# Nine plain units in place of eleven, and the extra weight jobs on a rhythm of 11 slots

## The chip, the cores and the metric

The kernel runs on one core of one Trainium2 chip. The metric is the device time of one execution in microseconds (us). Before the change three runs gave 1226.11, 1227.10 and 1228.48 us, median 1227.1 us. All times "at" something are counted from the start of the profiled span.

## The reference, cut to what matters

```python
# x: 2304 tokens x 512, the output of a chunked attention (chunks of 64, 8 heads of 64)
h = np.maximum(x @ w_in, 0.0)              # first layer: 512 x 2048
x = h * h @ w_out                          # 2048 x 512
p = domain_probs / (domain_probs.sum(-1, keepdims=True) + 1e-09)   # 2304 x 4
out = np.zeros((N, D))
for e in range(4):                         # second layer, four experts
    h = np.maximum(x @ w1[e], 0.0)         # 512 x 1024
    out += p[:, e:e + 1] * (h @ w2[e])     # 1024 x 512
```

Everything is float32. The kernel gets that from the matrix engine by splitting each operand into a high and a low part and adding three products (high by high, high by low, low by high).

## The kernel before, in words

**Two stages.** The first 488 us are the attention and the first layer (`mlp`, steps of 384 or 512 tokens, numbered by the loop variable `r`). The rest is the second layer. Its work is cut into 48 units: three groups of tokens (`sp`), and in each group 16 units `m` (four experts, four column blocks of 256). A unit has seven slots `u`. In each slot `c_unit` (L579) does six matmuls of 384 columns for the first product of the layer; I call them c0 to c6.

**Two kinds of unit.** Both compute the first product by a seven-product scheme of Strassen's kind, which needs sums of weight blocks. The second product is done in one of two ways. A plain unit (`n < PLAIN`) does it directly in the next unit's slots 0 to 5: `plain_unit` (L700), six groups of six matmuls of 512 columns; the order of the groups is t = 3, 4, 5, 0, 1, 2. Group t = 3 needs block A21 of the hidden layer, which is made last: L646 (VectorE adds), L648 (ScalarE, high part), L611 (VectorE, low part, `low`). The other units use seven products there as well: `d_unit` (L683), 63 matmuls of 256 columns.

**Where the weight sums come from.** Sums and splits of weights are made once, stored to DRAM (`kept`) and loaded again by later units. There are three makers. (1) `job` (L457) runs during the first layer, at the steps in `JOBS`: it loads a raw block, makes four sums on GpSimd (L472) and four high/low splits (L479 ScalarE, L481 VectorE or GpSimd), and stores them (L486). Its `yield` numbers are half steps to wait. (2) A plain unit makes the first weights of a plain unit to come: `w1_raw` (loads, L452), `w1_add` (sums, L506), `w1_split` (L543 ScalarE, L544 GpSimd), `w1_keep` (store, L547); its second weights need no sums: `w2_raw` (L499), `w2_split` (L555, L556). (3) `w1_extra` (L513) makes, within the plain units, the first weights of units 11 to 15. It is a small program over its own slots s: loads at s = 0 into the single buffer `rawx`, sums (L521, GpSimd) at the slots in `EXTRA_SUMS`, splits (L526 ScalarE, then L527) at the slots in `EXTRA_PARTS`, store (L530) at `EXTRA_KEEP`.

**What sets the order.** Nothing is scheduled by a tool: each engine runs its instructions in the order in which the loops emit them, and waits at each for what it needs. In a slot the order is: c_unit, c_finish, w1_split, w1_keep and w1_raw (u = 1), w2_split (u = 2, 3), w2_raw (u = 3), w1_add (u = 3 to 6), w1_extra, then plain_unit and its move L722. All transfers of this stage are issued by SyncE (SP), in one queue.

**c_finish (L624)** moves the products on. ScalarE copies b after c0 and c2 and d after c3 (L629). c4 overwrites b, so it waits for the copy after c2; c6 waits for L636, which reads b after c4. L638 and L640 finish block A11, L636 and L640 finish A22.

```python
    EXTRA_SUMS = {4: 0, 5: 1, 6: 2, 10: 3}                 # L533: slot -> which sum
    EXTRA_PARTS = {3: (1, nc.vector), 9: (2, nc.vector), 12: (0, nc.gpsimd), 13: (3, nc.vector)}
    EXTRA_KEEP = 14
                    if 0 <= 7 * n + u - 14 * i <= EXTRA_KEEP:       # L1045, i = 0 to 4
                        w1_extra(11 + i, 7 * n + u - 14 * i)
```

Of the kernel before, what the change touches and what calls it, by code (L numbers as in the profile page):

```python
# [33 lines left out]
NSUP = 3  # L34
LAG_A = 2
UOFF = [1, 3, 5, 16, 8, 17, 18, 19]
JOBS = [23, 26, 29, 32, 35, 44, 47, 50, 53, 56, 64, 67, 70, 73, 76, 79]
PLAIN = 11
SWAP = 67


# [5 lines left out]
def tile_kernel(ctx, tc, q, k, v, moe_w_in, moe_w_out, moe2_p, moe2_w1, moe2_w2, out):  # L47
    nc = tc.nc
# [317 lines left out]
    for sp in range(NSUP):  # L366
        if sp < NSUP - 1:
            r = [starts[2 * sp] + i * P for i in range(3)] + [starts[2 * sp + 1] + i * P for i in range(3)]
        else:
            r = [starts[NB - 1] + i * P for i in range(3)] + [starts[2 + i] + HALF for i in range(3)]  # L370
# [66 lines left out]
    NU = E * NP  # L437
# [16 lines left out]
                in_=moe2_w1[e, h0 * 2 * P:h1 * 2 * P, f0:f0 + P].rearrange("(k p) f -> p k f", p=P),  # L454
            )

    def job(which, n):  # L457

        e, j = divmod(n, NP)
        r = late["jb"].tile([P, 7, 2 * P], F32, tag="raw", name="jraw", bufs=2)  # L460
# [9 lines left out]
        yield 4  # L470
        for o, a, b, op in SUMS[which]:
            nc.gpsimd.tensor_tensor(out=r[:, o], in0=r[:, a], in1=r[:, b], op=op)  # L472
        yield 4
        c = NW // 4
        done = []
        for part in range(4):
# [53 lines left out]
                nc.sync.dma_start(out=kept[1, n][:, z], in_=ar[:, o:o + NW].bitcast(F32))  # L530

    rawx = {}
    EXTRA_SUMS = {4: 0, 5: 1, 6: 2, 10: 3}  # L533
    EXTRA_PARTS = {3: (1, nc.vector), 9: (2, nc.vector), 12: (0, nc.gpsimd), 13: (3, nc.vector)}
    EXTRA_KEEP = 14

    def w1_split(n, part):
        c = NW // 2
# [67 lines left out]
    def plain(n):  # L606
        return n < PLAIN

# [117 lines left out]
    def d_move(n, t, what):  # L726
# [10 lines left out]
        if what == "B":  # L737
            b = pb[n, t, 1]
            fresh = j == 0 or n == PLAIN
            if fresh and t == 2:  # L740
# [112 lines left out]
    with tc.manual_schedule():  # L853
# [57 lines left out]
        for i in range(4):  # L911
            early[SWAP + 5 + i] = [(w1_add, (0, i))]
            early[LEAD + NS - 8 + i] = [(w1_add, (1, i))]
        work = [(2, i) for i in range(NU)]
        going = []

        def advance(half):
# [12 lines left out]
        for r in range(LEAD + NS + LAG):  # L930
# [7 lines left out]
            run_all(do(r, "load"))  # L938
            advance(2 * r)
            if r in JOBS:  # L940
                going.append([2 * r, job(*work[JOBS.index(r)])])
                advance(2 * r)
            if r < NTILE + LAG_A:
                if r < NTILE:
# [50 lines left out]
        for n in range(NQ + 2):  # L995
# [5 lines left out]
            for u in range(7):  # L1001
                ds = [(d, at) for d, at in ((n - 1, u), (n - 2, u + 7)) if PLAIN <= d < NQ]
                if n < NQ:
                    if u == 0 and PLAIN <= n + 1 < NQ:
                        w1_load(n + 1)
                    c_unit(n, u)
                    if n == u == 0:
# [5 lines left out]
                        late["o"] = {}  # L1013
                    if n == PLAIN and u == 0:
                        raw_pool.close()
# [26 lines left out]
                if u >= 3 and n + 2 < PLAIN:  # L1042
                    w1_add(n + 2, u - 3)
                for i in range(5):
                    if 0 <= 7 * n + u - 14 * i <= EXTRA_KEEP:  # L1045
                        w1_extra(11 + i, 7 * n + u - 14 * i)
                if 0 < n <= PLAIN and u < 6:
                    t = (u + 3) % 6
                    plain_unit(n - 1, t)
# [38 lines left out]
```

## Time and profile before

| what | value |
|---|---|
| median of three runs | 1227.1 us (1226.11 to 1228.48) |
| profiled execution | 1226.38 us |
| its span | 1224.5 us |
| TensorE busy / VectorE / ScalarE / GpSimd | 98% / 67% / 49% / 58% |
| matmuls, weight loads | 8047 each |
| granted TensorE clock, mean | 0.993 |
| DRAM traffic | 189.30 MB read, 63.44 MB written |

The profiled execution is 0.7 us below the median and inside the spread of the three runs. The profile's page gives shares over the whole span; the timeline gives instructions in order of time, merged where one engine repeats a line; a bracket names what ended the idle time before an instruction. PEld is the weight load of TensorE, which runs beside its matmuls.

### The profile page before, as it was taken

Reading aid. Unit: us, or ns where it says so; the run is one execution under the profiler, and the core shown is the slowest. Engines: PE = TensorE matmul, PEld = TensorE weight load, DVE = VectorE, ACT = ScalarE, POOL = GpSimd, SP = SyncE. Lnnn points to the kernel's source line nnn. Section 1 sums busy time; section 2 is a strip of 40 time slices with the busy share of each in tenths; the row PEclk is TensorE's granted clock in tenths of the full one; section 3 lists DMA queues with packets and bytes.
Section 4 is the critical chain, followed back from the end, with each engine's and each line's share of the span. In section 5 each row is a group of like instructions: output and inputs, shape, how many; then the busy total and the mean of one; then the engine's idle time right before and its main releaser. Section 6 shows DMA issues by size and latency. Waiting matters only on the chain.

```text
span 1224.5 us, 21396 instructions
## 1 busy us (share of the span) xinstructions
PE 1196.7 (98%) x8047; PEld 1111.0 (91%) x8047; DVE 826.0 (67%) x1379; ACT 602.7 (49%) x1221; POOL 714.7 (58%) x686
## 2 busy tenths in 40 slices
PE   7899999999999999999999999999999999999997
PEld 5798888889888988888988999999999999999996
DVE  6975667656747466455555777676767776767676
ACT  5654555534534345644442556454445654545453
POOL 3410057726745455777881667667756766566665
PEclk8999999999999999999999999999999999999999
DMA  9855023552453644577767668666666686666652
GB/s 212 191 115 155 20 86 119 184 189 86 172 199 102 207 155 151 212 257 256 267 232 300 260 253 297 266 252 256 245 248 258 246 293 241 241 241 249 248 227 112
DMA packets 136230, 254.12 MB, mean 208 GB/s; under 512 B 64960, under 2 KB 110016, under 8 KB 129984
## 3 DMA queue, kind: packets, MB, share of 16 engines
q1 hardware_dynamic: 133504, 252.12, 59.1%
q8 instruction: 63, 1.03, 0.3%
q10 hardware_dynamic: 2624, 0.66, 0.3%
q14 instruction: 39, 0.32, 0.1%
HBM read 189.30 MB, written 63.44 MB: 206 GB/s over the span
## 4 chain that ended last, share of the span: by engine, by line
PE 89%; DVE 6%; ACT 1%; DMA 1%; issue 1%; POOL 1%; SPq 0%; DVEq 0%; ACTq 0%; POOLq 0%
PE pst L596 23%; PE psa L691 21%; PE psa L333 15%; PE pst L300 9%; PE psa L708 8%; PE psh L300 6%; PE psh L596 4%; PE pst L276 1%; PE pst L220 1%; PE pst L235 1%; DMA v<-in_v 1%; PE pst L262 1%; DVE o L791 1%; DVE uw L747 1%; DVE o L790 0%
## 5 line engine op out<-in xcount | busy, mean ns | idle before, releaser
L596 PE MATMUL pst<-ar 128*128 128x384 f32 x1728 | 345.6, 336 | 2.0 <-DVE psh L636 1.7
L596 PEld LDWEIGHTS pst<-ar 128*128 128x128 f32 x1728 | 293.7, 188 | 7.7 <-DVE psh L636 2.0
L333 PE MATMUL psa<-ar 128*128 128x512 f32 (+1 forms) x960 | 219.4, 372 | 1.2 <-ACT ar L316 0.4
L333 PEld LDWEIGHTS psa<-ar 128*128 128x128 f32 x960 | 173.5, 188 | 27.4 <-DVE ar L317 2.0
L622 POOL TENSOR_TENSOR ar<-s,ar 128x384 fp32r<-128x384 f32 x148 | 151.3, 1034 | 68.9 <-ACT ar L621 67.4
L691 PE MATMUL psa<-w2x,ar 128*128 128x256 f32 x1197 | 160.1, 278 | 2.5 <-DVE uw L745 2.3
L691 PE MATMUL psa<-ar 128*128 128x256 f32 x1134 | 158.0, 283 | 1.8 <-DVE uw L741 0.7
L691 PEld LDWEIGHTS psa<-w2x,ar 128*128 128x128 f32 x1197 | 154.8, 188 | 4.2 <-DVE uw L745 2.5
L691 PEld LDWEIGHTS psa<-ar 128*128 128x128 f32 x1134 | 151.2, 188 | 4.1 <-DVE uw L747 1.9
L145 POOL TENSOR_TENSOR raw<-raw 128x512 f32<-128x512 f32 x32 | 34.4, 1073 | 180.4 <-DVE raw L144 73.3
L759 POOL TENSOR_TENSOR o<-o,x 128x256 f32<-128x256 f32 x104 | 82.7, 795 | 80.3 <-ACT x L755 78.0
L300 PE MATMUL pst<-ar 128*128 128x512 f32 (+1 forms) x576 | 127.2, 369 | 0.0
L300 PEld LDWEIGHTS pst<-ar 128*128 128x128 f32 x576 | 105.4, 188 | 14.3
L629 ACT COPY u<-pst 128x384 f32<-128x384 f32 x144 | 69.7, 484 | 94.3 <-PE pst L596 92.2
L640 ACT ACTIVATE ar<-psh 128x384 fp32r<-128x384 f32 x96 | 47.3, 493 | 137.9 <-DVE psh L636 74.6
L621 ACT CAST ar<-s 128x384 fp32r<-128x384 f32 x148 | 75.8, 513 | 73.0 <-DVE s L617 67.9
L708 PE MATMUL psa<-ar 128*128 128x512 f32 x396 | 102.5, 394 | 0.0
L747 DVE TENSOR_TENSOR uw<-psa,uw 128x512 f32<-128x512 f32 x111 | 73.3, 687 | 34.6 <-PE psa L691 21.2
L300 PE MATMUL psh<-ar 128*128 128x512 f32 (+1 forms) x384 | 89.7, 376 | 2.2 <-DVE ar L284 2.2
L708 PEld LDWEIGHTS psa<-ar 128*128 128x128 f32 x396 | 73.2, 188 | 11.7 <-DVE ar L611 0.3
L745 DVE TENSOR_TENSOR uw<-psa,uw 128x512 f32<-128x512 f32 x81 | 56.0, 691 | 40.1 <-PE psa L691 39.8
L300 PEld LDWEIGHTS psh<-ar 128*128 128x128 f32 x384 | 69.0, 190 | 10.8 <-DVE ar L284 2.3
(136 smaller groups left out, 1936.0 us busy)
## 6 DMA issues: line engine op xcount, KB each, us to landing
ar<-w1d SPq DMA_DIRECT2D x37, 1792.0 KB, 7.3
w2x<-w2d SPq DMA_DIRECT2D x38, 896.0 KB, 7.6
ar<-w2d SPq DMA_DIRECT2D x36, 896.0 KB, 8.1
w2d<-jsplit SPq DMA_DIRECT2D x64, 448.0 KB, 3.5
w1d<-ar SPq DMA_DIRECT2D x11, 1792.0 KB, 8.7
w1d<-ar SPq DMA_DIRECT2D x10, 896.0 KB, 6.1
raw<-in_moe_w_in SPq DMA_DIRECT2D x16, 512.0 KB, 4.5
raw<-in_moe_w_out SPq DMA_DIRECT2D x16, 512.0 KB, 5.0
```

Source lines behind the costliest of these rows:

```text
L300: nc.tensor.matmul(ph[:, :T], lhsT=w[:, kk, :], rhs=x[tb][:, kk, :], start=(kk == 0 and n == 0), stop=(kk == KD - 1 and n == 2),)
L333: nc.tensor.matmul(o, lhsT=w, rhs=y, start=(f == 0 and n == 0), stop=(f == G - 1 and n == 2))
L596: nc.tensor.matmul(p, lhsT=w[:, kk, :], rhs=y[:, kk, :], start=(kk == 0 and z == 0 and u in (0, 1, 3)), stop=(kk == 1 and z == 2 and u in ...
L621: nc.scalar.copy(h, st[n, nm])
L622: nc.gpsimd.tensor_tensor(out=l, in0=st[n, nm], in1=h.bitcast(F32), op=ALU.subtract)
L629: nc.scalar.copy(s, d if at == 3 else b)
L640: nc.scalar.activation(out=g[n][i][0], in_=c, func=AF.Relu)
L691: nc.tensor.matmul(p, lhsT=w, rhs=y, start=(k in (1, 7) and z == 0), stop=(k in (3, 4) and z == 2), skip_group_check=True,)
L708: nc.tensor.matmul(p, lhsT=w[:, ts], rhs=y[:, i, :], start=(i == 0 and z == 0), stop=(i == 1 and z == 2))
L745: nc.vector.tensor_tensor(out=uw, in0=b, in1=uw, op=ALU.add)
L747: nc.vector.tensor_tensor(out=uw, in0=pb[n, t, 0], in1=uw, op=ALU.add)
L759: nc.gpsimd.tensor_tensor(out=o1[:, :2 * P], in0=o1[:, :2 * P], in1=x, op=ALU.add)
```

## The change

Units 9 and 10 become seven-product units. Their second weights were made by `job` before as well; their first weights are now made by two more jobs, so that the list of jobs grows from 16 to 18. In the last third of the first layer the jobs start every second step (64, 66, ... 78) and not every third, and wait two half steps and not four between sums and splits. The extra sums for units 11 to 15 take 11 slots each and not 14, and begin with unit 1 and not unit 0; the part that GpSimd split is now split on VectorE.

```diff
-JOBS = [23, 26, 29, 32, 35, 44, 47, 50, 53, 56, 64, 67, 70, 73, 76, 79]
-PLAIN = 11
+JOBS = [23, 26, 29, 32, 35, 44, 47, 50, 53, 56, 64, 66, 68, 70, 72, 74, 76, 78]
+PLAIN = 9
...
-    def job(which, n):
+    def job(which, n, lag):
...
-        yield 4
+        yield lag
...
-    EXTRA_SUMS = {4: 0, 5: 1, 6: 2, 10: 3}
-    EXTRA_PARTS = {3: (1, nc.vector), 9: (2, nc.vector), 12: (0, nc.gpsimd), 13: (3, nc.vector)}
-    EXTRA_KEEP = 14
+    EXTRA_SUMS = {3: 0, 4: 1, 5: 2, 6: 3}
+    EXTRA_PARTS = {3: (1, nc.vector), 7: (2, nc.vector), 8: (0, nc.vector), 9: (3, nc.vector)}
+    EXTRA_KEEP = 10
...
-        work = [(2, i) for i in range(NU)]
+        work = [(2, i) for i in range(12)] + [(1, 9), (2, 12), (2, 13), (1, 10), (2, 14), (2, 15)]
...
-                going.append([2 * r, job(*work[JOBS.index(r)])])
+                going.append([2 * r, job(*work[JOBS.index(r)], 4 if r < 64 else 2)])
...
-                    if 0 <= 7 * n + u - 14 * i <= EXTRA_KEEP:
-                        w1_extra(11 + i, 7 * n + u - 14 * i)
+                    if 0 <= 7 * n + u - 7 - 11 * i <= EXTRA_KEEP:
+                        w1_extra(11 + i, 7 * n + u - 7 - 11 * i)
```

Before, an extra job always began in slot 0 of a unit. Now the five begin in unit 1 slot 0, unit 2 slot 4, unit 4 slot 1, unit 5 slot 5 and unit 7 slot 2. I name each by the unit that it serves (the job for 11, for 12, ...). Three places of the order matter to the prediction.

**ScalarE in unit 0.** The names: `raw` are raw weights, `u` the copies of b and d, L526 the split of an extra part. Before:

```order
L629 COPY u_5018<-pst 128x384
L555 CAST ar<-raw_4209 128x512
L526 CAST ar<-rawx 128x448
L640 ACTIVATE ar<-psh 128x384
L648 ACTIVATE ar<-pst 128x384
```

and now:

```order
L629 COPY u_5062<-pst 128x384
L555 CAST ar<-raw_4215 128x512
L640 ACTIVATE ar<-psh 128x384
L648 ACTIVATE ar<-pst 128x384
L656 ACTIVATE ar<-pst 128x384
```

The extra part is gone from unit 0.

**ScalarE in units 3 and 4, as changed.** From the copy of b after c0 of unit 3:

```order
L629 COPY u_5393<-pst 128x384
L543 CAST ar<-raw_5136 128x896
L526 CAST ar<-rawx 128x448
L640 ACTIVATE ar<-psh 128x384
L543 CAST ar<-raw_5136 128x896
L629 COPY u_5440<-pst 128x384
```

and from c4 of unit 3 on:

```order
L640 ACTIVATE ar<-psh 128x384
L526 CAST ar<-rawx 128x448
L648 ACTIVATE ar<-pst 128x384
L526 CAST ar<-rawx 128x448
L656 ACTIVATE ar<-pst 128x384
L526 CAST ar<-rawx 128x448
```

The job for 12 has its first part in slot 0 of unit 3, ahead of the copy after c2 (the second L629), and its other three in slots 4, 5 and 6, the middle one behind L648. In slot 4 of unit 4 the first part of the job for 13 stands in the same way between L640 and L648. On VectorE the matching L527 stands there between L636 and L646:

```order
L636 TENSOR_TENSOR psh<-pst,u_5604 128x384
L527 TENSOR_TENSOR ar<-rawx,ar 128x448
L722 SCALAR_TENSOR_TENSOR o<-psa,prob,o 128x512
L611 SCALAR_TENSOR_TENSOR ar<-psh,ar 128x384
L646 TENSOR_TENSOR pst<-pst,u_5584 128x384
L722 SCALAR_TENSOR_TENSOR o<-psa,prob,o 128x512
L611 SCALAR_TENSOR_TENSOR ar<-pst,ar 128x384 x2
```

Before, no extra part stood on VectorE between L636 and the second L611.

**SP around unit 4, as changed.** `w1d` and L547, L530 are stores of finished weights, `rawx` the loads of the job for 13:

```order
L530 DMA w1d_106<-ar 128x1792 x2
L547 DMA w1d_90<-ar 128x3584
L452 DMA raw_5562<-in_moe_w 128x4x128
L452 DMA raw_5562<-in_moe_w 128x2x128 x2
L452 DMA rawx<-in_moe_w 128x4x128
L452 DMA rawx<-in_moe_w 128x2x128 x2
L499 DMA raw_5608<-in_moe_w 128x2x512
```

Before, the loads of `rawx` stood right behind a store L530 and ahead of L547; here they stand behind both stores and behind the unit's own raw load, which waits for GpSimd.

## Rows read from the trace of the kernel before

**Rows 1.** The page: busy time of each engine, share of the span, instructions.
```profile
PE 1196.7 (98%) x8047; PEld 1111.0 (91%) x8047; DVE 826.0 (67%) x1379; ACT 602.7 (49%) x1221; POOL 714.7 (58%) x686
```

**Rows 2.** Instructions by line: one per plain unit (L656), one per seven-product unit (L659).
```profile
L656 ACT ACTIVATE ar<-pst x11: 487/492/495, 502.1 to 658.1; 128x384 fp32r<-128x384 f32 x11
...
L659 ACT ACTIVATE ar<-pst x37: 482/485/493, 673.7 to 1205.2; 128x384 fp32r<-128x384 f32 x37
```

**Rows 3.** Timeline of unit 0: start, us, engine line op, count [idle before].
```profile
496.49 0.49 ACT L629 COPY u<-pst 128x384 f32<-128x384 f32 x1
...
497.39 0.58 ACT L526 CAST ar<-rawx 128x448 fp32r<-128x448 f32 x1
...
498.00 1.61 DVE L527 TENSOR_TENSOR ar<-rawx,ar 128x448 fp32r<-128x448 f32 x1 [2.54 <-ACT ar L526]
...
500.15 2.38 PE L596 MATMUL pst<-ar 128*128 128x384 f32 x12 [1.65 <-DVE psh L636]
```

**Rows 4.** Timeline of unit 5 and the start of unit 6, from c6 of unit 4.
```profile
562.97 2.25 PE L596 MATMUL pst<-ar 128*128 128x384 f32 x12
...
565.68 0.94 ACT L543 CAST ar<-raw 128x896 fp32r<-128x896 f32 x1
...
567.74 0.57 DVE L638 TENSOR_TENSOR psh<-psh,u 128x384 f32<-128x384 f32 x1 [0.35 <-PE psh L596]
...
570.18 0.48 ACT L629 COPY u<-pst 128x384 f32<-128x384 f32 x1 [0.51 <-PE pst L596]
...
573.51 1.12 PEld L596 LDWEIGHTS pst<-ar 128*128 128x128 f32 x6
...
575.64 0.49 ACT L640 ACTIVATE ar<-psh 128x384 fp32r<-128x384 f32 x1 [2.04 <-DVE psh L636]
...
578.10 0.49 ACT L648 ACTIVATE ar<-pst 128x384 fp32r<-128x384 f32 x1 [1.96 <-DVE pst L646]
...
578.81 0.75 DVE L722 SCALAR_TENSOR_TENSOR o<-psa,prob,o 128x512 f32<-128x512 f32 x1 [0.74 <-PE psa L708]
...
579.48 0.55 DVE L611 SCALAR_TENSOR_TENSOR ar<-pst,ar 128x384 fp32r<-128x384 f32 x1
...
580.53 1.28 PEld L708 LDWEIGHTS psa<-ar 128*128 128x128 f32 x6
```

**Rows 5.** Timeline of unit 1: an extra part on VectorE beside a GpSimd split.
```profile
507.79 2.13 POOL L544 TENSOR_TENSOR ar<-raw,ar 128x896 fp32r<-128x896 f32 x1
...
509.18 1.22 DVE L527 TENSOR_TENSOR ar<-rawx,ar 128x448 fp32r<-128x448 f32 x1 [2.31 <-ACT ar L526]
...
571.74 0.63 DVE L527 TENSOR_TENSOR ar<-rawx,ar 128x448 fp32r<-128x448 f32 x1 [1.45 <-ACT ar L526]
```

**Rows 6.** Timeline of SP and ScalarE: stores, loads, and the first use of `rawx`.
```profile
549.54 1.03 SPq L530 DMA_DIRECT2D w1d<-ar  x2
...
558.32 0.57 ACT L526 CAST ar<-rawx 128x448 fp32r<-128x448 f32 x1 [0.35 <-DMA rawx<-in_moe_w]
...
571.90 1.43 SPq L452 DMA_DIRECT2D raw<-in_moe_w  x3
...
575.00 0.37 SPq L499 DMA_DIRECT2D raw<-in_moe_w  x1
...
580.83 1.03 SPq L530 DMA_DIRECT2D w1d<-ar  x2
...
590.84 0.57 ACT L526 CAST ar<-rawx 128x448 fp32r<-128x448 f32 x1 [1.59 <-DMA rawx<-in_moe_w]
```

**Rows 7.** DMA issues at 571 to 576, then 556 to 561 us: KB, us to landing.
```profile
raw<-in_moe_w SPq DMA_DIRECT2D x1, 256.0 KB, 2.8
...
raw<-in_moe_w SPq DMA_DIRECT2D x1, 256.0 KB, 8.4
```

**Rows 8.** Timeline of the first layer: a step that made TensorE wait.
```profile
322.26 2.78 PE L333 MATMUL psa<-ar 128*128 128x384 f32 x12 [0.35 <-ACT ar L316]
```

**Rows 9.** Windows, 398 to 420 us: busy PE, PEld, DVE, ACT, POOL, clock, DMA share, GB/s.
```profile
398.00:420.00 22.00, 22.00 (x129) 22.00 (x128) 11.75 (x19) 8.62 (x19) 9.43 (x11) 1.00 0.62 209
```

## The prediction

> **What bounds the kernel now.** I read the page first, then the lines of the second layer, then its timeline unit by unit, then SP and the transfers. The page says that TensorE is busy 98% of the span [rows 1]; so the time changes only if matmuls go, or if TensorE waits more or less than it does. Where it waits, a look at the timeline tells: hardly in a plain unit, and at one place early in unit 0. The other engines are busy 49 to 67%, but each runs in its own order, so an instruction that waits holds up those behind it. What counts is therefore when four results of a unit are due.
>
> The calendar of a plain unit comes from unit 5 [rows 4]. The twelve matmuls from 562.97 are c6 and the next c0, so unit 5 starts at about 564.0; I give all times from a unit's start U. The first split of raw weights (L543) begins at +1.7, L638 at +3.7, the copy of b after c2 (L629) runs from +6.2 to +6.6, and the weights of c4, which needs it, are loaded from +9.5: 2.9 us to spare. L640 begins at +11.6, L648 at +14.1 (ends +14.6), the last move L722 at +14.8, and L611 (low part of A21) ends at +16.0. The first weights of group t = 3 are loaded at +16.5, and the low part is the third of its weights, one matmul step of 0.23 each (1.39 for six), so +17.0. A21 thus has 1.9 us to spare in its high part and 1.0 in its low one. These two margins are what the change eats.
>
> **What goes: two plain units.** One instruction per unit gives the period: (658.1 - 502.1) / 10 = 15.60 us for plain units, (1205.2 - 673.7) / 36 = 14.76 for the others [rows 2]. Two units of 0.84 make **-1.7 us** (bounds -1.5 and -1.8, as the second figure holds a few waits of its own).
>
> **What goes: the stall in unit 0.** There the extra part's L526 ran to 497.97, L527 took 1.61 us behind it, L636 came after, and TensorE had waited 1.65 us when c6 began at 500.15 [rows 3]. The copy that L636 needs was done at 496.97. Without the extra part L636 can run while c5 runs, and the stall goes: **-1.7** (bounds 0, if something else is late there, and -1.9). What is late next is L648 and L611 for group t = 3, but they follow L636 and move with it.
>
> **What is added in the first layer.** Two jobs more, each with four sums, four ScalarE and four VectorE or GpSimd splits, three loads and four stores. TensorE was busy 22.00 of 22.00 us where the job of step 64 ran, with ScalarE at 8.6 and GpSimd at 9.4 [rows 9]; a job every two steps adds half as much again. I take **0**, hidden by the 22 - 12 us that VectorE, the busiest of the three, has left; the bound above is two or three steps where a split stands before the first layer's own work on VectorE, as where TensorE waited 0.35 us and more [rows 8]. That was beside conversions, which have ended by step 65.
>
> **What moves: the extra jobs.** The first part (s = 3) waits for the loads of s = 0. Before, loads and part stood at the same places of a unit, and part one had 1.59 us of wait at the worst [rows 6] in slot 3, where it cost TensorE nothing. Now both wander. Also, a part on VectorE next to a GpSimd split takes 1.22 us, ending with the rest of the other's 2.13, and not 0.63 [rows 5]; so each part that falls behind an L544 or L556 costs VectorE what is left of that.
>
> *The job for 11* has parts in slots 0, 1, 2 of unit 2. L527 in slot 0 ends behind L544, at +5.3 and not +3.7; the chain L722, L638, L640, L543 shifts by 2.2 us, and two more parts get in L556's way. TensorE loses about nothing (copy after c2 at +8.7, due +9.5), but the second L556 ends 2.7 us later, at +13.7, and SP, which issued L499 behind it at +11.0 [rows 6], issues it at +13.7, and the store and loads of the job for 12 behind that.
>
> *The job for 12, slot 0 of unit 3.* From L530 to the first use of `rawx` it took 558.32 - 549.54 = 8.8 us, and 10.0 in the other job [rows 6]. L530 now goes at +14.1 of unit 2, with a raw load of 0.5 MB just ahead (0.8 more): the loads land at 14.1 + 8.8 + 0.8 = 23.7, which is +8.1 of unit 3. ScalarE stands at L526 from +2.6. Behind it come L526 0.57, L527 0.63, L722 0.75, L638 0.57, L640 0.49, L543 0.94 and L629 0.48 [rows 4 to 6], 4.4 us together: the copy ends at about +12.4 where the weights of c4 were due at +9.5. I take **+2.7**, as neighbours on one engine overlap a little (bounds 0, if the loads land by +5, and +3.9 with the 10.0).
>
> *The job for 12, slots 4 to 6 of unit 3.* Two parts now stand before L611 of A21. Each puts L526 and L527, some 1.2 to 1.3 us, between L640 and L646, and between L648 and the last L722. Chained with the durations above: L640 to +12.1, L526 12.6, L527 13.3, L722 14.0, L611 14.6, L646 15.1, L648 15.6, L526 16.1, L527 16.7, L722 17.5, L611 18.0 against +17.0: 1.0 late, and up to 2.3 if both meet a GpSimd instruction. **+1.4**.
>
> *The job for 13, slot 4 of unit 4.* SP issues its loads behind the unit's raw load, which waits for L544 until +7.9 (571.90) [rows 6]. A raw load lands 2.8 us after its issue when the queue is empty, 8.4 when a store is ahead [rows 7]; here the stores L530 and L547 are ahead, and 0.5 MB of raw load. So they land between +12.1 and about +16.6; I take +15.8, near the row with the store. ScalarE is at L526 from +12.1. Then L526, L527, L722, L611, L646, L648 take 0.57 + 0.63 + 0.75 + 0.55 + 0.56 + 0.49 and some 0.3 of waits, 3.85 in all: A21's high part is there at +19.6, due +16.5. **+3.1** (bounds 0.5 and 3.9).
>
> Here a rule could speak otherwise. In the rows a load queued behind a store lands 5.6 us later than one alone [rows 7]. The Trainium skill ("DMA: Bandwidth & Descriptors", section "Issuing engines are not separate DMA queues") says that transfers from the issuing engines run on the same 16 DMA engines and interleave; a load would then share and not queue, both loads would be about in time, and the sum would be that of the second rival. The same page ("Queues, rings and completion order") has descriptors of one queue taken in ring order, and all of these are in SP's queue; with that the rows agree, and the sum stands.
>
> *The jobs for 14 and 15* put one part each before L611 of A21: 0.1 us inside the margin without a GpSimd instruction in the way, up to 0.9 outside with one: **+0.5** for both (bounds 0 and 1.2). (The part that GpSimd gives up to VectorE is one of these; GpSimd's own time is not on the path.)
>
> **The sum:** -1.7 - 1.7 + 0 + 2.7 + 1.4 + 3.1 + 0.5 = +4.3. From the profiled execution's 1226.4 that is **1230.7 us**. The median of the runs is 0.7 above that execution, within their spread of 2.4, and I add nothing for it. What a measurement of this kernel tells from no change is about 0.2%, 2.45 us: below 1224.65 is faster, above 1229.55 slower.
>
> **The rivals.** *One load in time.* If unit 2 does not hold SP's queue back, the loads of the job for 12 land at +5 of unit 3 and the 2.7 falls away: 1228.0, no change. For it: raw loads do land in 2.8 us when the queue is empty; against: the part in slot 0 does meet L544.
>
> *No queue at all (ends not slower).* The mechanism is in unit 3 slot 0 and unit 4 slot 4: if loads share the engines with the stores ahead, they land by +5 and about +13. It decides at +5.3 in unit 3 and +12.1 in unit 4; earlier costs nothing. Then only 0.5 of the 5.8 is left, and the sum is -1.0; with the parts at their unhindered 0.63 (1.0 for 1.4, 0 for 0.5) it is -1.9: 1224.5. For it: 2.8 us alone; against: 8.4 behind a store.
>
> *The first layer stalls.* Job splits in 384-wide steps come before L312 and L316, two or three times [rows 8]: +2, 1232.7.
>
> *Unit 0 keeps its stall*, since the copies behind L543 are what is late there: +1.7, 1232.4.
>
> **How the numbers follow.** The forecast has 0.40: its own range, 1229 to 1233, is nearly all slower (0.36, and 0.04 no change). One load in time 0.24 (0.22 no change, 0.02 slower). No queue 0.21, with its centre just beyond the bound (0.15 faster, 0.06 no change). First layer 0.08, slower. Unit 0 0.07 (0.04 slower, 0.03 no change). That makes 0.15 faster, 0.35 no change, 0.50 slower. The range from 1224.2 to 1233.0 leaves out about 0.08 on either side: the lower half of the third case, the upper end of the first layer's.
>
> **What would show it.** After the change unit 0 should be 1.7 us shorter, with L636 before 498. The unit period must be 15.6 in units 1, 2, 5 and 8. L629 after c2 of unit 3 must come behind an L526 that waited for a DMA some 5 us, and c4 there must wait for it; group t = 3 must wait for L611 at the end of unit 3 and for L648 at the end of unit 4, behind an L526 that waited 3 to 4 us for `rawx`. TensorE must be without gaps from 398 to 484 us. I am wrong if these two L526 do not wait, or if VectorE and ScalarE catch up before c4 and group t = 3 are due.

## The result: 0.57% slower, and the profile after

The changed kernel takes **1233.3 us** (median of 5 runs, 1231.87 to 1235.55), the kernel before 1226.1 us beside it (5 runs, 1225.53 to 1228.48): ratio 1.0057, 95% interval 1.0046 to 1.0069. That is slower, as forecast, but by 7.2 us where the sum said 4.3, and just above the range (1224.2 to 1233.0). The profiled execution took 1231.87 us; it is the shortest of the five, which matters further down.

The page of the kernel after, its span and its engines (beside [rows 1]):

```profile
span 1229.7 us, 21586 instructions
...
PE 1197.9 (97%) x8101; PEld 1113.0 (91%) x8101; DVE 846.6 (69%) x1396; ACT 607.6 (49%) x1239; POOL 718.6 (58%) x695
```

TensorE's busy time grew by 1.2 us and the span by 5.2 (1224.5 before); so most of what is new is time in which it stands still. The instructions by line, one per plain unit (L656) and one per seven-product unit (L659), as in [rows 2]:

```profile
L656 ACT ACTIVATE ar<-pst x9: 486/492/494, 499.8 to 633.8; 128x384 fp32r<-128x384 f32 x9
...
L659 ACT ACTIVATE ar<-pst x39: 482/483/493, 649.0 to 1210.6; 128x384 fp32r<-128x384 f32 x39
```

A plain unit now takes (633.8 - 499.8) / 8 = 16.75 us on average, and took 15.60; the others take (1210.6 - 649.0) / 38 = 14.78, and took 14.76. So nearly all of the loss lies in the plain units. To see in which, I take from the traces the time from the first matmul of c0 of one unit to that of the next, in us. The last column is a second profile of the changed kernel (told among the experiments):

| stretch | before | after | difference | second profile |
|---|---|---|---|---|
| first layer, up to unit 0 | 488.64 | 488.32 | -0.32 | 487.43 |
| unit 0 | 12.69 | 10.75 | -1.94 | 10.75 |
| units 1 and 2 | 31.41 | 31.37 | -0.04 | 31.37 |
| unit 3 | 15.64 | 20.56 | **+4.92** | 20.87 |
| unit 4 | 15.64 | 16.69 | **+1.05** | 15.76 |
| unit 5 | 15.64 | 18.12 | **+2.48** | 20.99 |
| units 6 to 8 | 46.92 | 46.93 | +0.01 | 46.93 |
| units 9 to 12 | 60.35 | 58.94 | -1.41 | 58.94 |
| units 0 to 12 together | 198.29 | 203.36 | +5.07 | 205.61 |
| unit 13 to the end | 537.52 | 538.05 | +0.53 | 538.58 |

A wait for group t = 3 of unit 3 falls into unit 4 by this count, one for group t = 3 of unit 4 into unit 5. The last row is a small cost that the forecast did not have. It is there in every profile with nine plain units or fewer (537.93 us and more), and in neither profile with eleven (537.52, and 537.53 in run 1 below); what causes it was not tested.

*Unit 0.* The stall of [rows 3] is gone: L636 runs at 497.23, and from c4 on 24 matmuls run without a gap, c6 among them (one row of the timeline):

```profile
495.82 4.45 PE L596 MATMUL pst<-ar 128*128 128x384 f32 x24 [0.36 <-ACT u L629]
496.18 0.49 ACT L629 COPY u<-pst 128x384 f32<-128x384 f32 x1
...
497.23 0.57 DVE L636 TENSOR_TENSOR psh<-pst,u 128x384 f32<-128x384 f32 x1 [2.08 <-ACT ar L555]
```

*Unit 3* begins at 530.43. The timeline of the kernel after, from SP's stores for 11 to c4 of unit 3:

```profile
528.52 0.94 SPq L530 DMA_DIRECT2D w1d<-ar  x2
529.50 4.24 SPq L452 DMA_DIRECT2D rawx<-in_moe_w  x3
...
539.37 0.57 ACT L526 CAST ar<-rawx 128x448 fp32r<-128x448 f32 x1 [6.32 <-DMA rawx<-in_moe_w]
539.97 0.76 DVE L527 TENSOR_TENSOR ar<-rawx,ar 128x448 fp32r<-128x448 f32 x1 [8.08 <-ACT ar L526]
...
543.10 0.48 ACT L629 COPY u<-pst 128x384 f32<-128x384 f32 x1
...
543.64 2.29 PE L596 MATMUL pst<-ar 128*128 128x384 f32 x6 [3.32 <-ACT u L629]
```

This is the chain that was foreseen: L526 waits 6.32 us for the loads, which have landed at +8.94 of the unit; the copy L629 after c2 stands behind it, and c4 waits 3.32 us for the copy. What was not foreseen stands in the last row: those six matmuls take 2.29 us where six usually take 1.2. The windows of the same kernel show why (columns as in [rows 9]):

```profile
398.00:420.00 22.00, 22.00 (x129) 22.00 (x128) 12.96 (x20) 10.33 (x21) 14.47 (x17) 1.00 0.84 279
536.00:543.00 7.00, 4.33 (x21) 3.45 (x20) 3.03 (x6) 1.68 (x3) 0.74 (x1) 1.00 0.86 336
543.10:546.50 3.40, 2.86 (x8) 2.75 (x9) 1.66 (x3) 1.91 (x5) 3.22 (x3) 0.50 0.00 1
```

For 3.41 us from 543.10 on, right at the end of the wait, the granted clock is 0.50, the lower of its two levels (1.2 GHz). Of these 3.41 us 2.87 lie behind the wait; with matmuls about twice as long in them, unit 3 loses its wait and then, by estimate, 1.4 us more. The first row is the first layer where the jobs now start every second step: TensorE is busy 22.00 of 22.00 us, as in [rows 9].

*Units 4 and 5.* The timeline from group t = 3 of unit 3 to that of unit 4 (unit 4 begins at 550.99):

```profile
553.42 1.20 PE L708 MATMUL psa<-ar 128*128 128x512 f32 x4 [0.76 <-DVE ar L611]
...
559.94 2.00 SPq L452 DMA_DIRECT2D raw<-in_moe_w  x3
561.98 1.53 SPq L452 DMA_DIRECT2D rawx<-in_moe_w  x3
...
567.49 0.57 ACT L526 CAST ar<-rawx 128x448 fp32r<-128x448 f32 x1 [3.32 <-DMA rawx<-in_moe_w]
...
570.43 0.49 ACT L648 ACTIVATE ar<-pst 128x384 fp32r<-128x384 f32 x1 [2.37 <-DVE pst L646]
...
570.97 1.78 PE L708 MATMUL psa<-ar 128*128 128x512 f32 x6 [2.08 <-ACT ar L648]
```

The low part of A21 (L611) is late at the end of unit 3, and at the end of unit 4 the high part (L648) is late behind the L526 of the job for 13. That is what the forecast named. The rows also show when these loads were issued: at 561.98, which is +11.0 of the unit, behind the raw load, which SP issued at 559.94, when the GpSimd split L544 had ended.

### The profile page after: what moved, and what is told of

It reads as the page before. It is cut to its first block, busy times and chain, and to the rows that moved or that the text cites. A ratio compares the mean times of both kernels' runs of the same rounds, so it can differ in the third digit from the quotient of the medians.

```text
span 1229.7 us, 21586 instructions
## 1 busy us (share of the span) xinstructions
PE 1197.9 (97%) x8101; PEld 1113.0 (91%) x8101; DVE 846.6 (69%) x1396; ACT 607.6 (49%) x1239; POOL 718.6 (58%) x695
## 3 DMA queue, kind: packets, MB, share of 16 engines
q8 instruction: 64, 1.05, 0.3%
## 4 chain that ended last, share of the span: by engine, by line
PE 47%; DVE 5%; issue 2%; POOL 1%; DMA 1%; ACT 1%; SPq 0%; DVEq 0%; POOLq 0%; ACTq 0%
PE psa L691 21%; PE pst L596 20%; PE psh L596 3%; PE psa L708 3%; DMA rawx<-in_moe_w 1%; DVE uw L747 1%; DVE o L790 1%; DVE s L617 1%; SPq L452 0%; DVE o L791 0%; DVE ar L611 0%; POOL ar L544 0%; DVE o L773 0%; ACT a L644 0%; DVE psh L636 0%
## 5 line engine op out<-in xcount | busy, mean ns | idle before, releaser
L596 PE MATMUL pst<-ar 128*128 128x384 f32 x1728 | 346.8, 336 | 3.7 <-ACT u L629 3.7
L596 PEld LDWEIGHTS pst<-ar 128*128 128x128 f32 x1728 | 293.7, 189 | 8.5 <-ACT u L629 4.4
L622 POOL TENSOR_TENSOR ar<-s,ar 128x384 fp32r<-128x384 f32 x156 | 158.7, 1029 | 76.6 <-ACT ar L621 75.5
L333 PEld LDWEIGHTS psa<-ar 128*128 128x128 f32 x960 | 173.6, 188 | 27.5 <-DVE ar L317 2.0
L691 PE MATMUL psa<-w2x,ar 128*128 128x256 f32 x1260 | 168.4, 278 | 2.6 <-DVE uw L745 2.4
L691 PE MATMUL psa<-ar 128*128 128x256 f32 x1197 | 167.0, 283 | 2.2 <-DVE uw L741 0.8
L691 PEld LDWEIGHTS psa<-w2x,ar 128*128 128x128 f32 x1260 | 162.9, 188 | 4.3 <-DVE uw L745 2.6
L691 PEld LDWEIGHTS psa<-ar 128*128 128x128 f32 x1197 | 159.7, 188 | 4.6 <-DVE uw L747 1.9
L759 POOL TENSOR_TENSOR o<-o,x 128x256 f32<-128x256 f32 x110 | 87.2, 792 | 86.1 <-ACT x L755 83.8
L621 ACT CAST ar<-s 128x384 fp32r<-128x384 f32 x156 | 79.9, 513 | 77.1 <-DVE s L617 71.9
L640 ACT ACTIVATE ar<-psh 128x384 fp32r<-128x384 f32 x96 | 47.3, 493 | 141.0 <-DVE psh L636 72.0
L629 ACT COPY u<-pst 128x384 f32<-128x384 f32 x144 | 69.8, 485 | 88.0 <-PE pst L596 85.7
L747 DVE TENSOR_TENSOR uw<-psa,uw 128x512 f32<-128x512 f32 x117 | 77.4, 688 | 35.2 <-PE psa L691 20.2
L745 DVE TENSOR_TENSOR uw<-psa,uw 128x512 f32<-128x512 f32 x87 | 60.1, 691 | 43.5 <-PE psa L691 43.2
L708 PE MATMUL psa<-ar 128*128 128x512 f32 x324 | 84.9, 397 | 2.8 <-ACT ar L648 2.1
L481 POOL TENSOR_TENSOR jsplit<-jraw,jsplit 128x448 fp32r<-128x448 f32 x36 | 45.7, 1271 | 47.7 <-ACT jsplit L479 47.7
```

Source lines behind the costliest of these rows:

```text
L333: nc.tensor.matmul(o, lhsT=w, rhs=y, start=(f == 0 and n == 0), stop=(f == G - 1 and n == 2))
L596: nc.tensor.matmul(p, lhsT=w[:, kk, :], rhs=y[:, kk, :], start=(kk == 0 and z == 0 and u in (0, 1, 3)), stop=(kk == 1 and z == 2 and u in ...
L621: nc.scalar.copy(h, st[n, nm])
L622: nc.gpsimd.tensor_tensor(out=l, in0=st[n, nm], in1=h.bitcast(F32), op=ALU.subtract)
L629: nc.scalar.copy(s, d if at == 3 else b)
L640: nc.scalar.activation(out=g[n][i][0], in_=c, func=AF.Relu)
```

## The experiments

The theory to test was this: the loss is made where a ScalarE split (L526) stands ahead of a result that is due and waits for loads, and where splits crowd L611; the shorter rhythm put it there. Fewer plain units and more jobs in the first layer cost nothing. Two things were open: why the loads land late, and why the median lies above the sum. All runs "beside" are of the kernel before on the same chip. "The block" is units 0 to 12 (198.29 us before, 203.36 after).

**1. Only unit 0 freed.** The kernel before, with its 14-slot rhythm begun in unit 1:

```diff
-                    if 0 <= 7 * n + u - 14 * i <= EXTRA_KEEP:
-                        w1_extra(11 + i, 7 * n + u - 14 * i)
+                    if 0 <= 7 * n + u - 7 - 14 * i <= EXTRA_KEEP:
+                        w1_extra(11 + i, 7 * n + u - 7 - 14 * i)
```

> The kernel before, with its five extra jobs of 14 slots begun in unit 1 and not in unit 0; 11 plain units and 16 jobs as before. Theory (the extra part in unit 0 delays L636 there, and nothing else is late behind it): c6 of unit 0 no longer waits, unit 0 is 1.9 us shorter as it was with the whole change, the five jobs cost TensorE nothing since they still begin in slot 0 of a unit; 1.9 us faster than before, ratio 0.9984. Rival (the stall only moves, to unit 1 or to the end of the plain units, where the last job now ends in unit 10): within 0.5 us of before.

Measured: 1225.75 us (11 runs, 1222.9 to 1226.81), ratio 0.9995 (0.9987 to 1.0004). In the trace unit 0 takes 10.75 us, units 1 to 9 take 15.64 to 15.73, and the block 196.56: 1.73 less than before. So the trace shows the gain of the theory at its place, and the measured times do not: 1.9 us would be a ratio of 0.9984, just outside the interval. The runs lie in two groups (five at 1222.9 to 1223.6, six at 1225.75 to 1226.8); the 23 of the kernel before spread from 1224.34 to 1227.94 without such a gap. In the profiles the half-clock stretches of the first 45 us add up to 10.2, 13.7 or 17.1 us; they differed between two executions of one kernel, too (13.7 and 10.2 for the changed one). That this is what spreads the runs was not shown. A part of 1.7 us is here read from the trace and not from the median.

**2 to 4. The late jobs' parts moved back.** In the changed kernel the parts of both jobs, of 12 alone, or of 13 alone are split later, so that the loads have three slots more:

```diff
-        if s in EXTRA_SUMS:
+        sums, parts = (LATE_SUMS, LATE_PARTS) if n in LATE else (EXTRA_SUMS, EXTRA_PARTS)
+        if s in sums:
...
+    LATE = (12, 13)                                  # or (12,), or (13,)
+    LATE_SUMS = {4: 0, 5: 1, 6: 2, 7: 3}
+    LATE_PARTS = {6: (1, nc.vector), 7: (2, nc.vector), 8: (0, nc.vector), 9: (3, nc.vector)}
```

> The whole change, but in the jobs for 12 and 13 the first part is split three slots later (slots 6 to 9 of the job and not 3, 7, 8, 9, the sums at 4 to 7 and not 3 to 6), so that ScalarE comes to it when the loads have landed; same loads, same work. Theory (ScalarE, in order, waits for late loads): both waits for rawx on ScalarE are under 0.5 us, the wait at c4 of unit 3 (3.5 us) and at group t = 3 after unit 4 (2.2 us) go, and with the first the stretch of half TensorE clock (1.5 us); what stays is 1 to 2 us at group t = 3 after unit 3, where four parts now stand in a row. 5 to 6.5 us faster than the change, ratio to before 0.999 to 1.001. Rival (the parts crowd VectorE and ScalarE whenever they come, the loads are not what is late): at most 1.5 us faster than the change, ratio 1.004 or more.

> As the run with both, but only the job for 12 is changed so; the job for 13 keeps its first part at slot 3. Theory: the wait at c4 of unit 3 goes with its 3.5 us, and no stretch of half clock follows there; ScalarE in unit 4 still waits 2 to 3.5 us for the loads of the job for 13 and TensorE some 2 us at the next group t = 3. 3.5 to 5 us faster than the change, ratio 1.001 to 1.003. Rival (the clock falls wherever, and the wait in unit 4 grows by what unit 3 saved, since stores pile up ahead of its loads): less than 2.5 us faster than the change.

> As the run with both, but only the job for 13 is changed so. Theory: c4 of unit 3 waits 3.5 us as with the change and the clock halves right after it, so the half clock belongs to that wait; the 2.2 us after unit 4 go. 2 to 2.5 us faster than the change, ratio 1.0035 to 1.005. Rival (the half clock belongs to the second wait): no stretch at half clock in the second layer, 4 us or more faster than the change.

| moved | median us (runs) | ratio, interval | unit 3 | unit 4 | unit 5 | block | half clock in it |
|---|---|---|---|---|---|---|---|
| both | 1226.21 (12) | 1.0007, 0.9997 to 1.0018 | 15.64 | 17.48 | 15.64 | 199.45 | none |
| 12 alone | 1229.61 (6) | 1.0031, 1.0019 to 1.0044 | 15.64 | 17.70 | 18.43 | 199.86 | none |
| 13 alone | 1231.52 (5) | 1.0044, 1.0031 to 1.0057 | 20.87 | 16.45 | 16.78 | 202.40 | 3.41 us, in unit 3 |

The three expectations held in the main; two numbers with 12 alone came out just beyond what was said (a ratio of 1.0031 for 1.001 to 1.003, and 3.65 us of wait on ScalarE in unit 4 for 2 to 3.5). Each late load owns its unit: unit 3 is whole again when the job for 12 waits three slots longer, unit 5 nearly so when the job for 13 does. The longest waits of TensorE after 528 us, first with 12 alone moved, then with 13 alone (four new lines in the file move L596, L611, L629 and L648 to L600, L615, L633 and L652):

```profile
PE psa L712 <- ACT ar L652: 2.4, 1, 2.4
```

```profile
PE pst L600 <- ACT u L633: 3.4, 1, 3.4
```

The 2.4 us brought no half clock with it, the 3.4 us did. With both moved, units 4, 6 and 7 are still 1.84, 1.41 and 0.87 longer than 15.64, which eats the gains. In units 4 and 7 the parts that were moved back crowd A21: TensorE waits 1.50 and 0.28 us for the low part (L615). In unit 6 it is the next late load, that of the job for 14 (timeline, with both moved; L527 is the split that was L526):

```profile
590.15 0.56 ACT L527 CAST ar<-rawx 128x448 fp32r<-128x448 f32 x1 [4.39 <-DMA rawx<-in_moe_w]
...
591.15 1.31 PE L600 MATMUL pst<-ar 128*128 128x384 f32 x6 [1.15 <-ACT u L633]
```

**5. Nineteen jobs, four extra jobs on the old rhythm.** Nine plain units; the weights for 11 come from one job more in the first layer (the list `work` grows by it):

```diff
-JOBS = [23, 26, 29, 32, 35, 44, 47, 50, 53, 56, 64, 66, 68, 70, 72, 74, 76, 78]
+JOBS = [23, 26, 29, 32, 35, 44, 47, 50, 53, 56, 64, 66, 68, 70, 72, 74, 76, 78, 80]
...
-    EXTRA_SUMS = {3: 0, 4: 1, 5: 2, 6: 3}
-    EXTRA_PARTS = {3: (1, nc.vector), 7: (2, nc.vector), 8: (0, nc.vector), 9: (3, nc.vector)}
-    EXTRA_KEEP = 10
+    EXTRA_SUMS = {4: 0, 5: 1, 6: 2, 10: 3}
+    EXTRA_PARTS = {3: (1, nc.vector), 9: (2, nc.vector), 12: (0, nc.gpsimd), 13: (3, nc.vector)}
+    EXTRA_KEEP = 14
...
-                for i in range(5):
-                    if 0 <= 7 * n + u - 7 - 11 * i <= EXTRA_KEEP:
-                        w1_extra(11 + i, 7 * n + u - 7 - 11 * i)
+                for i in range(4):
+                    if 0 <= 7 * n + u - 7 - 14 * i <= EXTRA_KEEP:
+                        w1_extra(12 + i, 7 * n + u - 7 - 14 * i)
```

> Nine plain units as in the change, but a third job more in the first layer (for unit 11), so that only four extra jobs remain, on the old rhythm of 14 slots, begun in unit 1: each begins in slot 0 of a unit, as before the change. Theory (what the change lost is the place of the extra parts: loads asked for in slots 4 and 1, parts before the copy after c2 and before A21): units 1 to 8 all last 15.64 us, no half clock in the second layer, the first layer ends where it did (488.3 to 488.7), and the whole keeps the two gains of the change, 1.9 for unit 0 and 1.7 for two units: 1222 to 1223 us against 1226.1, ratio about 0.997. Rival (nine plain units or the denser jobs of the first layer cost something by themselves, such as memory traffic of the seven-product units that now all load from DRAM, or the job at step 80): ratio 1.000 or more, with waits in the first layer's last steps or in units 9 to 11.

Measured: **1222.48 us** (7 runs, 1221.57 to 1224.58) against 1226.34 beside, ratio 0.9969 (0.9958 to 0.9981). Unit 0 takes 11.10, units 2 to 9 take 15.64 each, the block 195.02 (3.27 less than before), the first layer ends at 488.80, and there is no half clock in the second layer. In the timeline the first part of an extra job now waits 0.34 us and not 6.32:

```profile
541.20 0.57 ACT L526 CAST ar<-rawx 128x448 fp32r<-128x448 f32 x1 [0.34 <-DMA rawx<-in_moe_w]
```

So fewer plain units and 19 jobs are worth what the steps of the forecast said (-1.7 and -1.7), and all the rest was the price of how the extra jobs were placed. This run also has one extra job less and gives GpSimd its part back, so it does not show the rhythm alone; that the part alone wins nothing is shown by run 6. This version is faster than both kernels.

**6. One part back on GpSimd.** The changed kernel with one word changed:

```diff
-    EXTRA_PARTS = {3: (1, nc.vector), 7: (2, nc.vector), 8: (0, nc.vector), 9: (3, nc.vector)}
+    EXTRA_PARTS = {3: (1, nc.vector), 7: (2, nc.vector), 8: (0, nc.gpsimd), 9: (3, nc.vector)}
```

> The change, but part 0 of an extra job is split on GpSimd again, as before the change. Theory (the wait at the end of unit 3, 1.05 us in the trace, comes from the three extra splits that stand on VectorE before the second L611): with one split less there, unit 4, which begins with that wait, lasts 15.6 to 16.0 and not 16.69 us; unit 3 (20.56) and unit 5 (18.12) stay within 0.5 us of what they were, since their waits stand in ScalarE for loads. Total 0.5 to 1.2 us shorter in the trace, within the scatter of the runs. Rival (it is ScalarE, or the two engines that get in each other's way while both split): unit 4 stays at 16.5 us or more.

Measured: 1237.7 us (one run; 1226.34 beside). The wait for L611 is gone as expected, unit 4 takes 15.64; but nothing is won, the block takes 207.74. Units 3 and 5 went to 22.71 and 21.39, and that half of the expectation missed; SP issued the loads for 12 at +15.4 of unit 2 here, and at +14.7 in the changed kernel. The rows of the timeline that end the waits of units 3 and 4:

```profile
545.88 2.29 PE L596 MATMUL pst<-ar 128*128 128x384 f32 x6 [4.02 <-ACT u L629]
...
575.37 2.67 PE L708 MATMUL psa<-ar 128*128 128x512 f32 x6 [3.85 <-ACT ar L648]
```

Behind the first the clock was half for 6.83 us, behind the second for 3.41. The second shows a trade: the loads for 13 land when they land; a unit 4 that loses nothing at its start comes to its own group t = 3 earlier and waits there longer, and the longer wait also brought the half clock. Here the 1.05 us of unit 4, once saved, were lost again in unit 5.

**7. The loads in a queue of their own.** In the changed kernel ScalarE issues the extra jobs' loads:

```diff
-            w1_get(rawx[n], n)
+            w1_get(rawx[n], n, nc.scalar)
```

> The change, but the loads of the extra jobs are issued by ScalarE and not by SP, so that they stand in a queue of their own and behind none of SP's stores and waits. Theory (the loads for 12 and 13 are late because they stand behind SP's waits and stores in one queue): they are issued 2 to 6 us earlier and land within 3 to 6 us; L526 in unit 3 and in unit 4 waits for no load over 1.5 us, units 3 and 5 last 16.5 us or less each (20.56 and 18.12 in the change), no half clock behind c4 of unit 3, and the whole is 4.5 to 7 us under the change. Rival (the 16 DMA engines are what the loads wait for, whichever queue they come from): the loads land at about the same time as in the change, 8 to 9 us after their issue, and units 3 and 5 stay within 1.5 us of 20.56 and 18.12.

Measured: 1237.68 us (one run); units 3 and 5 take 23.93 and 16.84, the block 208.39. The transfers issued from 524 to 531 us (KB, us to landing), and the timeline of unit 3:

```profile
w1d<-ar SPq DMA_DIRECT2D x2, 896.0 KB, 6.8
w1d<-ar SPq DMA_DIRECT2D x1, 1792.0 KB, 13.2
...
rawx<-in_moe_w ACTq DMA_DIRECT2D x1, 256.0 KB, 14.1
rawx<-in_moe_w ACTq DMA_DIRECT2D x2, 128.0 KB, 13.8
```

```profile
528.25 2.94 ACTq L452 DMA_DIRECT2D rawx<-in_moe_w  x3
...
542.92 0.56 ACT L526 CAST ar<-rawx 128x448 fp32r<-128x448 f32 x1 [9.12 <-DMA rawx<-in_moe_w]
```

For the loads for 12 the theory fell: issued at +12.6 of unit 2 (+14.7 in the changed kernel) and behind nothing in their queue, they still took 14 us, as long as the store L547 that ran at the same time (13.2, and 9.9 in the changed kernel). The 8 to 9 us of the rival missed as well. In SP's queue the loads stood ahead of that store; here the two ran together, and both took longer. From 528 to 543 us the DMA engines were busy 0.84 of the time:

```profile
528.00:543.00 15.00, 13.13 (x66) 11.47 (x64) 3.52 (x7) 2.76 (x6) 4.50 (x5) 1.00 0.84 316
```

The loads for 13 were issued 6.3 us earlier in unit 4 and landed 2.0 us earlier, at +14.5; group t = 3 waited 0.77 us for L648 and not 2.08. The loads for 14 were issued late, because ScalarE comes to them late in its own order, and unit 6 lost 2.4 us.

**8. The changed kernel again**, for a second profile.

> The change once more, for a second profile. Theory (the costs of the second layer belong to the order of the work, and what scatters from execution to execution is TensorE's clock): the same units are long, by the same amounts to 0.4 us (unit 3 20.6, unit 4 16.7, unit 5 18.1, unit 9 16.0), half clock again for about 3.4 us behind the wait before c4 of unit 3, and what the total differs by from 1231.87 us lies in the first 50 us and in stretches of half clock. Rival (the lateness of the loads scatters): unit 3 or unit 5 differs by over 1 us without a difference in the clock.

Measured: 1233.79 us; the block took 205.61 (table above). Units 3 and 9 repeat to 0.3 us, units 4 and 5 do not, where the theory wanted 0.4: it missed there. In the timeline the loads for 13 were there at +17.2 of unit 4 (+16.5 in the first profile), group t = 3 waited 3.73 us for L648 and not 2.08, and the clock fell behind it:

```profile
567.66 0.56 ACT L526 CAST ar<-rawx 128x448 fp32r<-128x448 f32 x1 [4.99 <-DMA rawx<-in_moe_w]
...
571.13 2.93 PE L708 MATMUL psa<-ar 128*128 128x512 f32 x6 [3.73 <-ACT ar L648]
```

```profile
570.80:574.10 3.30, 2.97 (x7) 2.40 (x8) 1.33 (x4) 1.86 (x4) 2.15 (x3) 0.50 0.13 55
```

The rival has a part in this: the wait is 1.65 us longer, 0.93 of it because unit 4 lost only 0.12 at its start here (the trade of run 6), and the rest because the loads were 0.7 us later in the unit. With both half clocks this execution took about what the median says; the first profile, with one, was the shortest of its five. That this is what lifts the median rests on these two profiles alone. Why unit 4 lost 0.12 here and 1.05 there I did not settle.

**9. The stores for 11 and 12 left out.** All extra jobs in place, but the first two store nothing; units 11 and 12 get their weights from two jobs more in the first layer (steps 60 and 80; the list `work` grows by them):

```diff
-JOBS = [23, 26, 29, 32, 35, 44, 47, 50, 53, 56, 64, 66, 68, 70, 72, 74, 76, 78]
+JOBS = [23, 26, 29, 32, 35, 44, 47, 50, 53, 56, 60, 64, 66, 68, 70, 72, 74, 76, 78, 80]
...
-        if s == EXTRA_KEEP:
+        if s == EXTRA_KEEP and n > 12:
```

> The change with all its extra jobs in their places (loads, sums, splits), but the jobs for 11 and 12 store nothing; units 11 and 12 get their first weights from two jobs more in the first layer. So 1.8 MB of stores less stand ahead of the loads for 12 and for 13. Theory (the loads are late because the 16 DMA engines are busy with these stores, from whichever queue): the loads for 12 land 3 to 5 us after their issue, before +4.5 of unit 3, L526 in slot 0 of unit 3 waits under 2 us, unit 3 lasts 15.6 to 16.5 us (20.56 in the change) without half clock behind it; the loads for 13 land 1 to 3 us earlier than +16.5 of unit 4; the wait for L611 at the end of unit 3 (1.0 us) stays, since the splits stay. Together 1226 to 1229 us. Rival (the loads are late because SP issues them late, behind its waits for L556 and L544, and take long by themselves): they land 7 to 9 us after issue again, and unit 3 lasts over 19.5 us.

Measured: 1235.96 us (one run), for a reason outside the question: the first layer ended at 495.66, 7.3 us late. The block took 199.47, 3.9 less than in the changed kernel. Unit 3 takes 15.64; the wait for L611 at its end stays, as expected (unit 4 takes 17.39). The loads for 12, in the list of transfers and in the timeline:

```profile
rawx<-in_moe_w SPq DMA_DIRECT2D x1, 256.0 KB, 4.1
rawx<-in_moe_w SPq DMA_DIRECT2D x2, 128.0 KB, 4.0
```

```profile
535.90 1.48 SPq L452 DMA_DIRECT2D rawx<-in_moe_w  x3
...
540.91 0.57 ACT L526 CAST ar<-rawx 128x448 fp32r<-128x448 f32 x1 [0.53 <-DMA rawx<-in_moe_w]
```

Issued at the same place of SP's order, they landed in 4.1 us and not in 9.1: for the job for 12 **the 1.8 MB of stores ahead are what made the loads late**, and the rival (late issue alone) is out.

For 13 the expectation missed: the loads should have landed 1 to 3 us earlier than +16.5, and they were there at +17.4 (unit 5 takes 18.41), though the two stores L530 were gone. The timeline, issue and first use:

```profile
564.57 1.48 SPq L452 DMA_DIRECT2D rawx<-in_moe_w  x3
...
570.84 0.57 ACT L526 CAST ar<-rawx 128x448 fp32r<-128x448 f32 x1 [3.56 <-DMA rawx<-in_moe_w]
```

Here the late issue, which the rival named, is the larger part. The loads were issued at +11.2 of the unit (+11.0 in the changed kernel), and ScalarE is free for the split at +13.2 in the changed kernel. From issue to use it took 5.5 us there, 6.7 in its second profile and 6.3 here, against 5.0 for the loads for 12 in this run, with no store ahead. So of the 3.32 us that this L526 waited in the first profile, an estimate from these rows gives 2.8 to the late issue and 0.5 to what stood ahead.

Of the 7.3 us that the first layer lost, some 5 were lost near the jobs at steps 60 and 64 (two waits of TensorE, 3.4 us together, and half clock for 3.41 us); the start of this execution had 3.4 us more of half clock than the profile of before. The timeline there:

```profile
414.98 0.57 ACT L479 CAST jsplit<-jraw 128x448 fp32r<-128x448 f32 x1 [4.94 <-DMA w2d<-jsplit]
...
418.34 3.97 PE L333 MATMUL psa<-ar 128*128 128x384 f32 x12 [2.40 <-ACT ar L316]
```

It is the same mechanism in another place: a job's ScalarE split waits 4.94 us for the store of an earlier split to leave its buffer, the first layer's own work on ScalarE stands behind it, TensorE waits, and its clock was half for 3.41 us from 419.7.

**10. Seven plain units, 22 jobs.** From run 5, two units further:

```diff
-JOBS = [23, 26, 29, 32, 35, 44, 47, 50, 53, 56, 64, 66, 68, 70, 72, 74, 76, 78, 80]
-PLAIN = 9
+JOBS = [23, 26, 29, 32, 35, 38, 44, 47, 50, 53, 56, 59, 62, 64, 66, 68, 70, 72, 74, 76, 78, 80]
+PLAIN = 7
...
```

The list `work` and the loop over the extra jobs follow.

> The version with 19 jobs carried two units further: seven plain units, 22 jobs in the first layer (steps 38, 59 and 62 more), three extra jobs on the old rhythm of 14 slots. Theory (a plain unit is worth 0.85 us, and a job in the first layer costs nothing as long as TensorE does not wait there): the first layer ends at 488 to 489 us and the whole is 1.7 us under the version with 19 jobs, 1220 to 1221.5 us, ratio to before about 0.9955. Rival (a job at step 38, 59 or 62 stands beside the conversions and the attention, where ScalarE, VectorE and GpSimd have no time left): TensorE waits 1 us or more in each, the first layer ends at 490 us or later, and the ratio is 0.997 or more.

Measured: 1241.28 us (4 runs, 1239.4 to 1242.06), ratio 1.0118 (1.0101 to 1.0135): the rival holds, but not for step 38. The first layer ends at 507.50, 19 us late: TensorE waited 12.2 us between 400 and 430 us and had half clock for 13.7 us there. The jobs of steps 59, 62 and 64 make their splits from 380 to 426 us. Around the job of step 38 (247 to 300 us) TensorE was busy without a gap. One row of the timeline shows the largest wait:

```profile
417.02 4.16 PE L333 MATMUL psa<-ar 128*128 128x384 f32 x12 [7.33 <-ACT ar L316]
```

ScalarE's splits (L479) waited up to 8.7 us there for stores of earlier splits. So a job is free where the change put its two, every second step from 64 on, and not in the steps just before. The plain units did give what was expected: the block took 193.54, 1.48 less than in run 5 (1.7 was said).

## Where the prediction was right, and which step of it failed

**Right: the sign, the four places and the two gains.** Unit 0 lost 1.94 us (forecast 1.7, bound 1.9). The two plain units are worth 1.41 + 0.39 = 1.80 in units 9 to 12, where unit 9 alone is 0.39 longer by the job for 15 (forecast 1.7, and 0.5 for the jobs for 14 and 15). (From unit 13 on 0.53 and 1.06 us of this are given back, which the forecast did not have.) The first layer cost 0: TensorE's waits from 250 to 489 us are 0.3 us, and were 0.4 before. The job for 11 cost nothing. L526 waited for loads in unit 3 and in unit 4, and L629, L648 and L611 stood behind as listed.

**Failed: the size of two terms of the sum, "the job for 12, slot 0 of unit 3" and "the job for 13, slot 4 of unit 4".**

| term | forecast (bounds) | first profile | second profile |
|---|---|---|---|
| two plain units | -1.7 | -1.80 | -1.80 |
| unit 0 | -1.7 | -1.94 | -1.94 |
| job for 12, slot 0 of unit 3 | +2.7 (0 to 3.9) | **+4.92** | **+5.23** |
| job for 12, slots 4 to 6 | +1.4 | +1.05 | +0.12 |
| job for 13, slot 4 of unit 4 | +3.1 (0.5 to 3.9) | +2.48 | **+5.35** |
| jobs for 14 and 15 | +0.5 | +0.39 | +0.39 |
| sum in units 0 to 12 | +4.3 | +5.07 | +7.32 |

(Units 1, 2 and 6 to 8 make up the last few hundredths.) The first term went beyond its upper bound in both profiles, the second in one, because the working priced a late result at its lateness and put what follows a wait at nothing, without a reason. In unit 3 the loads landed at +8.94 (forecast +8.1) and the copy was done at 543.58, +13.2 (forecast +12.4), so c4 waited 3.32 us and not 2.7; most of the rest of the 4.92, about 1.4 us of 1.6, is the half clock behind it. In unit 4 the loads landed at +16.5 and +17.2 (forecast +15.8); in the second profile the wait of 3.73 and the half clock behind it (about 1.5) make nearly all of the 5.35. The rows of before held no wait of that length in the second layer, so no row gave its price; but to let nothing follow a wait was a choice, and it is why the range ended too low.

**Failed as well: adding the two terms on A21.** Forecast as +1.4 and +3.1, they are not independent: what unit 4 loses at its start it need not wait at its end. The two together measured 3.53 and 5.47, against 4.5; without the half clock the second is about 4.0. That the first profile's sum (+5.07) comes so near to +4.3, and that its time lies inside the range, is partly luck: unit 3 was 2.2 us dearer than said, and these two 1.0 us cheaper.

**Why the loads were late.** The forecast put both down to SP's queue, by an issue that comes late and by stores ahead of it. For the job for 12 it was the 1.8 MB of stores (run 9), for the job for 13 mostly the late issue.

**The rule that was weighed.** The forecast read "share the engines" as "in time" and made a rival of it. Run 7 shows sharing, and it was worse: 14 us. The Trainium skill ("DMA: Bandwidth & Descriptors", section "Issuing engines are not separate DMA queues") says that transfers from all issuing engines run on the same 16 DMA engines and interleave, and that issuing from several saves only the time of the issue. With that the run agrees; what the forecast drew from it was wrong, since interleaving with 3.6 MB of stores is no faster than standing behind half of them. The rivals "one load in time", "no queue at all", "first layer stalls" and "unit 0 keeps its stall" are all excluded by the rows above.

**The median.** The forecast was set against one execution. In the profiles half clock behind the waits came once or twice, and the start of the kernel varies by itself; the second profile, with two, is the one that took the median's time.

## What to carry to other kernels

A work rhythm that is not a multiple of the loop's period walks through all places of the loop: look at the worst place that it reaches, not at the average engine share. A load was late here for two reasons: by the bytes of stores under way, from whichever queue (the job for 12), and by what its own queue waited for before it was issued (the job for 13). So count the megabytes ahead of it, and find the place of its issue, before moving its first use; and what waits for it on an in-order engine takes everything behind it along. Ask of a new wait on TensorE whether matmuls at half clock follow it (an estimated 1.4 to 1.7 us behind each of the waits of 3.3 to 3.9 us here), and don't add waits that one and the same late transfer causes.

## What the runs showed of the hardware that was not expected

- TensorE's clock fell to half after waits in the middle of a busy layer. With waits of 3.32 (first profile), 3.41 and 3.73 us (second profile), and 3.85 us (run 6) it was half for 3.41 us, with those of 4.02 (run 6) and 6.01 us (run 7) for 6.83. Behind the wait of 2.08 (first profile) and that of 2.4 (run 3) it stayed full, yet in the first layer a wait of 2.40 us in run 9, with others in the 12 us ahead of it, and one of 2.05 us in run 10, with no other in the 15 us ahead of it, were each followed by 3.41 us of half clock. So the length of one wait did not decide it alone.
- A wait removed upstream came back larger: run 6 freed 1.05 us in unit 4, and unit 5 went from 18.12 to 21.39, some 1.7 of it by half clock.
- The same loads took 4.1, 9.1 and 14.1 us to land: with no 1.8 MB store ahead, behind it in one queue, and beside it and a second one from another queue.
